# Attention with hash buckets and two MoE layers: weight conversions at other steps, and nine more useless products at the start

## The chip, the core and the metric

The kernel runs on one core of a Trainium2 chip. The metric is the device time of one execution in microseconds (us); smaller is better. Before the change three runs gave 1005.58, 1005.88 and 1007.04 us.

The core has a matrix engine (TensorE, PE in the rows; PEld are its weight loads), VectorE (DVE), ScalarE (ACT), GpSimd (POOL) and SyncE (SP), which only issues DMA transfers. Each engine takes its instructions in the order in which the program wrote them, and waits at an instruction until what it needs is there.

## The reference

```python
B, H, S, D = q.shape                                   # 2, 8, 768, 64
q_bits = (einsum('bhsd,dk->bhsk', q, proj) > 0)        # 6 hash bits of each row
k_bits = (einsum('bhsd,dk->bhsk', k, proj) > 0)
mask = q_bucket[:, :, :, None] == k_bucket[:, :, None, :]
scores = where(mask, q @ k.T / sqrt(D), -1e9)
attn = softmax(scores) @ v
x = attn as (1536 tokens, 512)
h = x @ w_in                                           # 512 -> 2048
x = where(h > 0, h, exp(min(h, 0)) - 1) @ w_out        # 2048 -> 512
p = domain_probs / sum                                 # 4 experts
out = sum over e of p[:, e] * (max(x @ w1[e], 0) @ w2[e])
```

`w_in` and `w_out` come as 64-bit floats and are turned into 32-bit ones on the chip, by integer operations on their two words.

## The kernel before

The attention stage works on eight pairs of heads, one after the other. A pair has 12 steps (six row blocks of 128 for each of its two heads); `g2` counts pairs and `i` steps, and the text writes (2, 3) for step 3 of pair 2. `att_step(u)` writes the instructions of one step in the order of the letters in `ORDER`: C combines the product sums of an earlier chunk, E is an exponential on ScalarE, T and t are transpositions on TensorE, Q the score products of two steps ahead, N the row minimum of these on VectorE, H, h, L and l split the transposed exponentials into a high part (ScalarE) and a low part (VectorE), W converts weights in step 3, M, m and d prepare a later pair, and V is the product with v. There is one score tile, so Q waits for the minimum of the step before.

What is prepared depends on the step. In steps 1 and 2 q of the next pair is transposed, in step 3 its hash bits are computed (the hashing step; in pair 0 step 5), in steps 10 and 11 k of the pair after is transposed. The transposed parts are split by GpSimd (`pool_split`) and brought to their places by SP.

Every third step, at i = 0, 3, 6 and 9, the combination C copies a product sum on ScalarE into the tile `t` (`t1` in the code, one buffer); GpSimd copies (L496) and adds (L500) from it. ScalarE can write it again only when GpSimd has done so. In steps 6 and 7 GpSimd multiplies the result of the last pair (L534) with the reciprocals `rx`, which SP loads in step 3 (`load_rx`, L526).

Beside this, three tiles of `w_in` and `w_out` are converted in the attention stage, tile m in the pairs 2m to 2m+3. `conv_w` gives the operations, each for the two halves 0 and 1: a (ScalarE, absolute value), x, s, t, n, m (VectorE: clamp L286, shift L287, merge L289, mask L291, low word L292) and p (GpSimd, addition L294); S0, S1 split the tile (GpSimd, L311 and L315). The table `PRE` says in which pair (relative to 2m) and step each is written; an entry of step 3 is written at W, all others at the end of the step behind the transfers of `loads_step`. The entry c gives the raw tile free, and `consumed` then issues the load of the next raw tile (L259 and L260) on SP at once. For tile 1, which has a place of its own, c does nothing.

At the start `first()` prepares pair 0. `warm(n)` writes n useless products of a zero tile. `WARM` holds their numbers; `WARM[1]` are those between the transpositions of k and of q. `emit_proj32` builds the small weight tile of the hashing step on GpSimd.

After the attention stage (at about 230 us) come the first MoE layer (L885) and the second (L1083 to L1136), both with TensorE working without a rest.

Of the kernel before, what the change touches and what calls it, by code (L numbers as in the profile page):

```python
# [37 lines left out]
def lsh_attention_moe_kernel(  # L38
# [36 lines left out]
    WA = 3  # L75
    ORDER = "CETHQtNRLhlWMmdV"
    ORDER0 = "EQNwTHtLhlWMmd"
    WARM = (28, 1, 8, 6, 4)
    GL = 0.0
    TAIL = "AoqpBpcpproppqppVVVncxkgogkqffzkffppppfffffffffffffffffoqfffffffff"  # L80

# [37 lines left out]
    def pair(g2):  # L119

        return g2 % B, g2 // B

    def load_qk(g2, nm):
        b, hp = pair(g2)
        t = st_p.tile([P, NJ, 2, D], F32, tag="s" + nm, name="s" + nm)
        x = {"k": k, "q": q}[nm][b, 2 * hp:2 * hp + 2]
        if g2:
            nc.sync.dma_start(out=t, in_=x.rearrange("h (p j) d -> p j h d", j=NJ))
        else:
            t = t.rearrange("p j h d -> p (j h d)").rearrange("p (h j d) -> p h j d", h=2, j=NJ)  # L130
            x = x.rearrange("h (p j) d -> p h j d", j=NJ)
            for js in (slice(0, NJ // 2), slice(NJ // 2, NJ)) if nm == "k" else (slice(0, NJ),):
                nc.sync.dma_start(out=t[:, :, js], in_=x[:, :, js])
        raws[g2, nm] = t
# [17 lines left out]
    def pool_split(hi, lo, x):  # L152
        nc.gpsimd.tensor_scalar(out=hi, in0=x, scalar1=1.0, scalar2=1.0, op0=ALU.mult, op1=ALU.mult)
        nc.gpsimd.tensor_tensor(out=lo, in0=x, in1=hi.bitcast(F32), op=ALU.subtract)
# [28 lines left out]
    def emit_proj32():  # L183
        nc.gpsimd.memset(pj32, 0.0)
        for i in range(2):
            r = slice(i * D, (i + 1) * D)
            for n, sign in enumerate((1.0, -1.0)):
                c0 = i * HB + n * NB
                nc.gpsimd.tensor_scalar(out=pj32[r, c0:c0 + NB], in0=prj[r], scalar1=sign, scalar2=1.0,
                                        op0=ALU.mult, op1=ALU.mult)  # L190
# [3 lines left out]
    def x_tiles(c):  # L194
        if c not in xh:
            xh[c], xl[c] = (xp.tile([P, NT], F32R, tag=f"x{n}{c}", name=f"x{n}{c}") for n in "hl")
        return xh[c], xl[c]
# [172 lines left out]
    def place(g2, nm, par):  # L370


        r = slice(par * D, (par + 1) * D)
        hi, lo = stg[nm + "h"][r].bitcast(F32), stg[nm + "l"][r].bitcast(F32)
        t = (ks_t if nm == "k" else qs_t)[sl(g2, par)].bitcast(F32)
        if nm == "k":
            parts = (t[0:D], hi.unsqueeze(1).to_broadcast([D, 2, S])), (t[D:P, 0], lo)
        else:
            parts = (t[0:D, 0], hi), (t[D:P, 0], hi), (t[0:D, 1], lo)
        for dst, src in parts:  # L380
            nc.sync.dma_start(out=dst, in_=src)
# [7 lines left out]
    def place_bits(g2, nm, par):  # L389
        for half in range(2):  # L390
            src, dst = bits_at(g2, nm, par, half)
            nc.sync.dma_start(out=dst.bitcast(F32), in_=src)
# [136 lines left out]
    def emit_fin(g2, half, by):  # L529
        b, hp = pair(g2)  # L530
        t0 = b * S + half * HS
        uu = u_t[g2][:, half * HS:(half + 1) * HS]
        eng = nc.gpsimd if by.space == uu.space else nc.vector
        eng.tensor_tensor(out=uu, in0=uu, in1=by, op=ALU.mult)  # L534
        pool_split(*(t[:, t0:t0 + HS] for t in x_tiles(hp)), uu)
# [8 lines left out]
    def emit_norm(g2, half, ps):  # L544
        for i in range(UC):
# [12 lines left out]
    EU = 0  # L558
    FIN_AT = (6, 7)
    SIDE_AT = (1, 6)  # L560
    PRE = ((0, 3, "a0"), (0, 6, "a1"), (0, 8, "x0"), (0, 10, "s0"), (1, 1, "t0"), (1, 2, "x1"), (1, 3, "s1"),
           (1, 6, "n0"), (1, 10, "t1"), (2, 1, "m0"), (2, 2, "n1"), (2, 3, "m1"), (2, 4, "p0 p1 c"), (2, 5, "S0"),
           (3, 4, "S1 C"))
    PRE = [{(2 * m + p, {3: 5, 6: 7}.get(i, i) if m + p == 0 else i): nm.split() for p, i, nm in PRE}
           for m in range(NPRE + 1)]
    PRE[NPRE][NPAIR - 1, 2] = PRE[NPRE].pop((NPAIR - 2, 5))
    MSTEP = [None] * PU
# [23 lines left out]
    def loads_step(g2, i):  # L591
        if g2 + 2 < NPAIR and i == L_AT:
            load_qk(g2 + 2, "k")
        if g2 + 1 < NPAIR:
            q0, b0, kq1, _ = (4, 5, 5, 0) if g2 == 0 else PLACE_AT
            if g2 == 0 and i == 1:
                place(g2 + 1, "k", 0)
            if i == q0:
                place(g2 + 1, "q", 0)
                if g2 and g2 + 2 < NPAIR:  # L600
                    load_qk(g2 + 2, "q")
            if g2 and i == b0:
                load_rx(g2 - 1)
            if i == b0:
                for nm in "kq":
                    place_bits(g2 + 1, nm, 0)
            if g2 == 0 and i == b0:
                load_v(1, 1)
                load_qk(2, "q")
            if i == kq1:  # L610
                for nm in "kq":
                    place(g2 + 1, nm, 1)
                    place_bits(g2 + 1, nm, 1)
        elif i == PLACE_AT[1]:
            load_rx(g2 - 1)
        if i == PLACE_AT[3] and g2 + 2 < NPAIR:
            place(g2 + 2, "k", 0)
        if i in FIN_AT and 0 < g2 < NPAIR:
            half = FIN_AT.index(i)
            emit_fin(g2 - 1, half, rx_t[g2 - 1][:, half * HS:(half + 1) * HS])  # L620
        if (g2, i) == (0, 0):
            for r in (slice(0, rows.start), slice(rows.stop, P)):
                nc.sync.dma_start(out=edge_t[r, 20:24], in_=consts[r])
            nc.sync.dma_start(out=dp.rearrange("p (b j) e -> p b j e", b=B),
                              in_=dprobs.rearrange("(b p j) e -> p b j e", b=B, j=NJ))
            loads()
        if g2 == 0 and i == 2:
            split_v(0, 1)
        if g2 + 1 < NPAIR and i in (0, 1) and (g2 or i == 0):
            load_v(g2 + 1, i)  # L630
        if (g2, i) == SIDE_AT:
            load_w(*SIDE)
        if g2 + 1 < NPAIR and i in V_AT:
            split_v(g2 + 1, V_AT.index(i))
# [11 lines left out]
    def first():  # L646
# [7 lines left out]

        warm(WARM[0])
        nc.vector.memset(ident, 0.0)
# [22 lines left out]
        for nm in "kq":  # L679
            los = []  # L680
            for half in range(2):
# [3 lines left out]
                if (nm, half) == ("k", 1):  # L685
                    warm(WARM[1])
                act()
# [36 lines left out]
        bits0("q")  # L724
        warm(WARM[2])
        return warm
# [3 lines left out]
        nc.sync.dma_start(out=t[1][D:KM, 1].bitcast(F32), in_=t[0][KM:KM + HB, 1].bitcast(F32))  # L730

    warm = first()
    emit_proj32()
    split_v(0, 0)
    for u in range(LQ):
        emit_qk(u)
        if u < LN:
            emit_min(u)
    warm(WARM[3])
    for u in range(LE):  # L740
# [11 lines left out]
    def pre_step(g2, i):  # L752
        for m in range(NPRE + 1):
            if (g2, i) in PRE[m]:
                if m not in pre:
                    pre[m] = pre_ops(m)
                for nm in PRE[m][g2, i]:
                    pre[m].pop(nm)()

    def att_step(u):  # L760
# [28 lines left out]
        if u == 0:  # L789
            ops["w"] = lambda: warm(WARM[4])  # L790
        if u == PROBS_AT:
# [613 lines left out]
```

## Time and profile before

| | us |
|---|---|
| median of three runs | 1005.88 |
| the profiled execution | 1006.43 |
| its span, first to last instruction | 1004.6 |
| TensorE busy | 998.1 |
| VectorE busy | 831.2 |
| GpSimd busy | 510.9 |
| ScalarE busy | 501.9 |

The profile is of one execution. A timeline row gives the start, the duration, the engine, the line of the code, the operation and what it writes and reads; in square brackets stands how long its engine was idle before it, and what ended that. A matmul's end is modelled, so a step's length is better read from the starts of weight loads.

### The profile page before, as it was taken

To read this page: it belongs to the slowest core of one execution; us is meant where nothing else is said; L and a number is where in the kernel's file an instruction comes from. 1 tells how busy PE (TensorE), PEld (TensorE's weight loads), DVE (VectorE), ACT (ScalarE), POOL (GpSimd) and SP (SyncE) were. 2 spreads that over 40 slices of the span, in tenths; PEclk is the share of its full clock that TensorE was granted. 3 is DMA by queue.
4 is the path that set the end of the run, shared out by engine and by line. 5 is a ranking of instruction groups with operands and counts; after the bars stand their busy time and mean duration, and the time that the engine had idled before them with its cause. 6 is when DMAs were issued, how large, how long until landed. Compare 5 with 4: busy or idle time off the path is not lost.

```text
span 1004.6 us, 16153 instructions
## 1 busy us (share of the span) xinstructions
PE 998.1 (99%) x5901; PEld 880.4 (88%) x5901; DVE 831.2 (83%) x1276; ACT 501.9 (50%) x988; POOL 510.9 (51%) x464
## 2 busy tenths in 40 slices
PE   9999999999999999999999999999999999999998
PEld 8898988898888888888789999999899999999988
DVE  7999999986898787624477788898998989989895
ACT  6989888886565444435433332333423334233331
POOL 5579797973364545412411244555445554455542
PEclk9999999999999999999999999999999999999999
DMA  8777776550222221100200020110201102011012
GB/s 208 168 169 187 164 163 142 127 171 1 84 84 84 84 80 46 42 1 23 71 25 1 12 95 11 43 43 11 95 12 42 43 11 96 11 44 42 1 43 84
DMA packets 72796, 71.97 MB, mean 72 GB/s; under 512 B 26194, under 2 KB 60790, under 8 KB 72718
## 3 DMA queue, kind: packets, MB, share of 16 engines
q1 hardware_dynamic: 72602, 70.95, 25.7%
q8 instruction: 47, 0.77, 0.3%
q14 instruction: 31, 0.25, 0.1%
q10 hardware_dynamic: 116, 0.00, 0.0%
HBM read 48.92 MB, written 3.21 MB: 52 GB/s over the span
## 4 chain that ended last, share of the span: by engine, by line
PE 51%; issue 5%; POOL 1%; ACT 0%; DVE 0%; POOLq 0%
PE l L1136 23%; PE a L1084 4%; PE r L1084 4%; PE a L1083 4%; PE r L1083 4%; PE a L1085 4%; PE r L1085 4%; POOL h L869 1%; PE l L1241 1%; PE l L885 1%; ACT w L313 0%; PE r L832 0%; PE r L831 0%; PE r L833 0%; DVE w L317 0%
## 5 line engine op out<-in xcount | busy, mean ns | idle before, releaser
L1136 PEld LDWEIGHTS l<-w,op 128*128 128x128 f32 x1932 | 241.0, 189 | 7.2
L1136 PE MATMUL l<-w,op 128*128 128x256 f32 x1932 | 243.0, 281 | 0.0
L1152 POOL TENSOR_TENSOR a<-a,temps 128x512 f32<-128x512 f32 x60 | 91.7, 1528 | 122.3 <-DVE a L1147 122.3
L1018 ACT ACTIVATE op<-hf 128x512 fp32r<-128x512 f32 x119 | 73.2, 626 | 137.7 <-DVE hf L1088 85.1
L885 PE MATMUL l<-h,w 128*128 128x512 f32 x576 | 140.1, 391 | 0.1
L869 POOL TENSOR_TENSOR h<-g,h 128x512 fp32r<-128x512 f32 x44 | 67.0, 1524 | 136.7 <-ACT h L865 95.5
L885 PEld LDWEIGHTS l<-h,w 128*128 128x128 f32 x576 | 107.7, 188 | 24.8 <-POOL h L869 1.3
L1022 DVE TENSOR_TENSOR op<-hf,op 128x512 fp32r<-128x512 f32 x119 | 123.3, 1050 | 4.8 <-ACT op L1018 4.7
L431 DVE TENSOR_SCALAR_CACHE_REDUCE mk<-s 128x768 f32<-128x768 f32 x96 | 91.5, 953 | 12.3 <-PE s L422 9.7
L464 DVE TENSOR_TENSOR ptl<-pt,pth 128x384 fp32r<-128x384 f32 x192 | 97.1, 547 | 1.1 <-ACT pth L467 1.0
L440 ACT ACTIVATE mk<-mk,mn 128x768 f32<-128x768 f32 x96 | 89.9, 937 | 10.8 <-DVE mk L431 10.4
L450 PE MATMUL pt<-cst,mk 128*128 128x128 f32 x576 | 93.9, 272 | 0.0
L467 ACT ACTIVATE pth<-pt 128x384 fp32r<-128x384 f32 x192 | 85.8, 487 | 7.2 <-PE pt L450 6.3
L421 PE MATMUL s<-ks,qs 128*128 128x512 f32 (+1 forms) x192 | 80.1, 439 | 1.3 <-DVE mk L431 1.2
L450 PEld LDWEIGHTS pt<-cst,mk 128*128 128x128 f32 x576 | 72.4, 140 | 8.6 <-ACT mk L440 0.4
L1084 PE MATMUL a<-xl,w 128*128 128x512 f32 x192 | 75.3, 392 | 0.0
L1084 PE MATMUL r<-xl,w 128*128 128x512 f32 x192 | 75.3, 392 | 0.0
L1083 PE MATMUL a<-xh,w 128*128 128x512 f32 x192 | 75.3, 392 | 0.0
L1083 PE MATMUL r<-xh,w 128*128 128x512 f32 x192 | 75.3, 392 | 0.0
L1085 PE MATMUL r<-xh,w 128*128 128x512 f32 x192 | 74.9, 390 | 0.0
L1085 PE MATMUL a<-xh,w 128*128 128x512 f32 x192 | 74.9, 390 | 0.0
L480 PE MATMUL pv<-pth,vs 128*128 128x384 f32 x192 | 72.7, 379 | 0.1
(193 smaller groups left out, 2131.4 us busy)
## 6 DMA issues: line engine op xcount, KB each, us to landing
raw<-in_moe_w_dram SPq DMA_DIRECT2D x32, 512.0 KB
raw<-in_moe_w_in_dram SPq DMA_DIRECT2D x15, 512.0 KB
raw<-in_moe_w_out_dram SPq DMA_DIRECT2D x15, 512.0 KB
ks<-kh SPq DMA_DIRECT2D x15, 384.0 KB
qs<-qh SPq DMA_DIRECT2D x30, 192.0 KB
sq<-in_q_dram SPq DMA_DIRECT2D x8, 384.0 KB
sv<-in_v_dram SPq DMA_DIRECT2D x16, 192.0 KB
pb<-pd SPq DMA_DIRECT2D x12, 256.0 KB
```

The costliest lines, as they stand in the source:

```text
L431: nc.vector.tensor_scalar(out=e_t[u], in0=s_t.pop(u)[:, 0:S], scalar1=MASKED, scalar2=None, op0=ALU.min, op1=ALU.min, accum_out=mn)
L440: nc.scalar.activation(out=e, in_=e, func=ACTF.Exp, bias=mn_t.pop(u), scale=-1.0, accum_out=sums_t[g2][:, j, par:par + 1])
L450: nc.tensor.transpose(pt[:, i * P:(i + 1) * P], e_t[u][:, kb * P:(kb + 1) * P], ident)
L464: nc.vector.tensor_tensor(out=lo, in0=pt, in1=hi.bitcast(F32), op=ALU.subtract)
L467: nc.scalar.activation(out=hi, in_=pt, func=ACTF.Copy)
L885: mm(ps, a, b_, start=(m == 0 and n == 0), stop=(m == GS[g] - 1 and n == 2))
L1022: e.tensor_tensor(out=lo, in0=x, in1=hi.bitcast(F32), op=ALU.subtract)
L1083: mm(ps, wh[:, cs], xh[c][:, ts], start=(c == 0), stop=False)
L1084: mm(ps, wh[:, cs], xl[c][:, ts], start=False, stop=False)
L1085: mm(ps, wl[:, cs], xh[c][:, ts], start=False, stop=(c == NC - 1))
L1136: mm(ps[:, tt * HD:(tt + 1) * HD], a[:, cs], b_[:, k_], start=(n == 0), stop=(n == 11))
L1152: nc.gpsimd.tensor_tensor(out=x, in0=x, in1=keep[nm], op=ALU.add)
```

## The change

Three things are changed. The table `PRE` has other steps for the operations of a conversion: the shift and the last low word leave the hashing step, the clamp leaves step 8; VectorE's ten operations now stand in steps 10 and 11 of the first pair, 1, 2, 4, 5, 10 and 11 of the second and 1 and 2 of the third. The additions p0, p1 and the release c move from step 4 of the third pair into step 3. At the start ten instead of one useless products stand between the transpositions of k and q. And the hashing weights are built in step 2 of pair 0 instead of behind `first()`.

```diff
-    WARM = (28, 1, 8, 6, 4)
+    WARM = (28, 10, 8, 6, 4)
...
-    PRE = ((0, 3, "a0"), (0, 6, "a1"), (0, 8, "x0"), (0, 10, "s0"), (1, 1, "t0"), (1, 2, "x1"), (1, 3, "s1"),
-           (1, 6, "n0"), (1, 10, "t1"), (2, 1, "m0"), (2, 2, "n1"), (2, 3, "m1"), (2, 4, "p0 p1 c"), (2, 5, "S0"),
+    PRE = ((0, 3, "a0"), (0, 6, "a1"), (0, 10, "x0"), (0, 11, "x1"), (1, 1, "s0"), (1, 2, "t0"), (1, 4, "s1"),
+           (1, 5, "n0"), (1, 10, "t1"), (1, 11, "n1"), (2, 1, "m0"), (2, 2, "m1"), (2, 3, "p0 p1 c"), (2, 5, "S0"),
            (3, 4, "S1 C"))
-    PRE = [{(2 * m + p, {3: 5, 6: 7}.get(i, i) if m + p == 0 else i): nm.split() for p, i, nm in PRE}
+    PRE = [{(2 * m + p, {3: 5, 6: 8}.get(i, i) if m + p == 0 else i): nm.split() for p, i, nm in PRE}
...
+        if (g2, i) == (0, 2):
+            emit_proj32()
...
     warm = first()
-    emit_proj32()
     split_v(0, 0)
```

VectorE in steps 1 to 3 of pair 2, before. mk is the row minimum that begins a step, ptl are the two low parts, raw and side the weights, hb the hash bits:

```order
L431 TENSOR_SCALAR mk,mn<-s 128x768
L464 TENSOR_TENSOR ptl<-pt_1227,pth 128x3x128
L464 TENSOR_TENSOR ptl<-pt_1237,pth 128x3x128
L291 TENSOR_SCALAR raw<-side 128x512
L431 TENSOR_SCALAR mk,mn<-s 128x768
L464 TENSOR_TENSOR ptl<-pt_1271,pth 128x3x128
L464 TENSOR_TENSOR ptl<-pt_1283,pth 128x3x128
L292 SCALAR_TENSOR_TENSOR raw<-raw 128x512
L406 TENSOR_SCALAR hb<-m,edge 128x384
```

And after, the same two steps:

```order
L431 TENSOR_SCALAR mk,mn<-s 128x768
L464 TENSOR_TENSOR ptl<-pt_1237,pth 128x3x128
L464 TENSOR_TENSOR ptl<-pt_1247,pth 128x3x128
L292 SCALAR_TENSOR_TENSOR raw<-raw 128x512
L431 TENSOR_SCALAR mk,mn<-s 128x768
L464 TENSOR_TENSOR ptl<-pt_1281,pth 128x3x128
L464 TENSOR_TENSOR ptl<-pt_1293,pth 128x3x128
L406 TENSOR_SCALAR hb<-m,edge 128x384
```

The low word L292 has moved out of the hashing step into step 2, and the mask that stood there has moved to step 11 of pair 1.

SP in steps 2 and 3 of pair 2, before. sq is a load of q, rx the reciprocals, the rows with hb bring hash bits, those of kh to ql the parts of the next head, raw are the weights:

```order
L381 DMA qs_126<-ql 64x768
L128 DMA sq<-in_q_dram 128x12x64
L526 DMA rx<-d 64x6x128 x2
L392 DMA ks_123<-hb 12x384 x2
L392 DMA qs_126<-hb 12x384 x2
L381 DMA ks_124<-kh 64x2x768
L381 DMA ks_124<-kl 64x768
L392 DMA ks_124<-hb 12x384 x2
L381 DMA qs_127<-qh 64x768 x2
L381 DMA qs_127<-ql 64x768
L392 DMA qs_127<-hb 12x384 x2
L259 DMA raw<-in_moe_w_in_dram 128x4x256
```

And after:

```order
L381 DMA qs_126<-ql 64x768
L128 DMA sq<-in_q_dram 128x12x64
L259 DMA raw<-in_moe_w_in_dram 128x4x256
L260 DMA raw<-in_moe_w_out_dram 128x1024
L526 DMA rx<-d 64x6x128 x2
L392 DMA ks_123<-hb 12x384 x2
```

The load of the next raw weights has moved from behind all transfers of step 3 to a place ahead of the first of them. The same happens in pair 6.

VectorE in steps 3 to 5 of pair 3, before; here the second weight tile is converted:

```order
L464 TENSOR_TENSOR ptl<-pt_1715,pth 128x3x128
L287 TENSOR_SCALAR w_1294<-w_1294 128x512
L406 TENSOR_SCALAR hb<-m,edge 128x384
L431 TENSOR_SCALAR mk,mn<-s 128x768
L464 TENSOR_TENSOR ptl<-pt_1754,pth 128x3x128
L464 TENSOR_TENSOR ptl<-pt_1764,pth 128x3x128
L431 TENSOR_SCALAR mk,mn<-s 128x768
L464 TENSOR_TENSOR ptl<-pt_1781,pth 128x3x128
```

And after:

```order
L464 TENSOR_TENSOR ptl<-pt_1724,pth 128x3x128
L406 TENSOR_SCALAR hb<-m,edge 128x384
L431 TENSOR_SCALAR mk,mn<-s 128x768
L464 TENSOR_TENSOR ptl<-pt_1762,pth 128x3x128
L464 TENSOR_TENSOR ptl<-pt_1772,pth 128x3x128
L287 TENSOR_SCALAR w_1308<-w_1308 128x512
L431 TENSOR_SCALAR mk,mn<-s 128x768
L464 TENSOR_TENSOR ptl<-pt_1790,pth 128x3x128
L464 TENSOR_TENSOR ptl<-pt_1800,pth 128x3x128
L291 TENSOR_SCALAR side<-w_1308 128x512
```

The shift L287 has moved from the hashing step to the end of step 4, and the mask L291 stands at the end of step 5 (before, of step 6).

## Rows read from the trace of the kernel before

**Rows 1.** The page: busy time, share of the span and instructions of each engine.

```profile
PE 998.1 (99%) x5901; PEld 880.4 (88%) x5901; DVE 831.2 (83%) x1276; ACT 501.9 (50%) x988; POOL 510.9 (51%) x464
```

**Rows 2.** Waits of weight loads, 16 to 225 us: total us, times, longest.

```profile
PEld s L421 <- DVE mk L431: 3.3, 9, 0.7
```

**Rows 3.** The same from 225 us to the end.

```profile
PEld l L885 <- POOL h L869: 1.3, 3, 0.5
PEld l L885 <- DVE a L904: 0.8, 2, 0.4
```

**Rows 4.** Timeline of weight loads: first score load of four steps of pair 2.

```profile
73.57 0.19 PEld L421 LDWEIGHTS s<-ks,qs 128*128 128x128 f32 x1
...
75.97 0.19 PEld L421 LDWEIGHTS s<-ks,qs 128*128 128x128 f32 x1
...
79.01 0.19 PEld L421 LDWEIGHTS s<-ks,qs 128*128 128x128 f32 x1
...
81.69 0.19 PEld L421 LDWEIGHTS s<-ks,qs 128*128 128x128 f32 x1 [0.56 <-DVE mk L431]
```

**Rows 5.** Timeline of VectorE: a shift in two places, two minima of pair 3.

```profile
39.45 0.42 DVE L287 TENSOR_SCALAR side<-side 128x512 int32<-128x512 int32 x1
...
94.92 1.23 DVE L287 TENSOR_SCALAR w<-w 128x512 int32<-128x512 int32 x1
...
110.49 0.96 DVE L431 TENSOR_SCALAR_CACHE_REDUCE mk<-s 128x768 f32<-128x768 f32 x1
...
112.56 0.96 DVE L431 TENSOR_SCALAR_CACHE_REDUCE mk<-s 128x768 f32<-128x768 f32 x1 [0.17 <-PE s L422]
```

**Rows 6.** Timeline of GpSimd in pairs 2, 3 and 6.

```profile
79.70 2.90 POOL L294 TENSOR_TENSOR side<-side,raw 128x512 f32<-128x512 f32 x2
...
87.20 1.01 POOL L534 TENSOR_TENSOR u<-u,rx 128x384 f32<-128x384 f32 x1 [0.99 <-DMA rx<-d]
...
94.86 1.00 POOL L500 TENSOR_TENSOR u<-u,t 64x384 f32<-64x384 f32 x1
...
108.53 1.28 POOL L315 TENSOR_TENSOR w<-side,w 128x512 fp32r<-128x512 f32 x1
...
192.97 2.57 POOL L294 TENSOR_TENSOR side<-side,raw 128x512 f32<-128x512 f32 x2
...
197.82 1.01 POOL L534 TENSOR_TENSOR u<-u,rx 128x384 f32<-128x384 f32 x1
...
205.41 1.01 POOL L500 TENSOR_TENSOR u<-u,t 64x384 f32<-64x384 f32 x1
```

**Rows 7.** Timeline of SP: issues in pairs 2 and 6.

```profile
80.46 2.04 SPq L526 DMA_DIRECT2D rx<-d  x2
...
93.01 0.45 SPq L259 DMA_DIRECT2D raw<-in_moe_w_in_dram  x1
...
191.68 1.51 SPq L526 DMA_DIRECT2D rx<-d  x2
```

**Rows 8.** Timeline of ScalarE: combinations at the first steps of pairs 3 and 7.

```profile
96.95 0.49 ACT L495 ACTIVATE t<-pv 128x384 f32<-128x384 f32 x1 [0.25 <-PE pv L481]
...
208.07 0.49 ACT L495 ACTIVATE t<-pv 128x384 f32<-128x384 f32 x1 [0.30 <-POOL vs L154]
```

**Rows 9.** First 5 us: busy time by engine; granted clock third from the end.

```profile
0.00:5.00 5.00, 4.01 (x33) 3.89 (x34) 1.44 (x6) 1.84 (x3) 1.50 (x10) 1.00 0.56 151
```

**Rows 10.** Timeline of the start, TensorE and one row of GpSimd.

```profile
0.99 3.17 PE L653 MATMUL pz<-pn 128*128 128x128 bf16 x28 [0.99 <-POOL pn L648]
...
6.42 1.54 PE L349 MATMUL pq<-cst,s 128*128 128x128 f32 x6 [0.76 <-DVE s L668]
7.62 1.63 PE L713 MATMUL hk<-kh,pj 128*128 128x384 f32 x4
...
14.69 0.88 PE L450 MATMUL pt<-cst,mk 128*128 128x128 f32 x6
...
10.14 0.79 POOL L189 TENSOR_SCALAR pj<-prj 64x6 f32<-64x6 f32 x4
```

## The prediction

> **What bounds the kernel now.** I read the busy shares first: TensorE is busy for 99% of the span [rows 1], so only two things can move the end: time in which TensorE stands still for another engine, and time in which its products run slowly. The waits of its weight loads over the attention stage come next. From 16 to 225 us the first score product of a step waits for VectorE's minimum nine times, 3.3 us in all [rows 2]; from 225 us to the end all named waits come to 2.1 us, none of them for a weight conversion of the attention stage [rows 3]. So what the attention stage gains or loses arrives at the end nearly whole, and the changed conversions lie in it.
>
> The step length is read from the first score weight load of each step [rows 4], or from VectorE's minima. A plain step takes 2.07 us (110.49 to 112.56 [rows 5]), a step with three transpositions for the next pair 2.40 (73.57 to 75.97), the hashing step 3.04 (75.97 to 79.01). The step after the hashing step takes 2.68 with a wait of 0.56 in it: the conversion in the hashing step of pair 2 made VectorE late, and TensorE paid one step later. In plain steps VectorE itself waits 0.17 for TensorE [rows 5]. It has that little room there, about half a microsecond in steps with transpositions, and about a whole one in the hashing step, if no conversion stands in it.
>
> A conversion has no fixed price. The shift of one 128x512 tile took 0.42 us at 39.45, and 1.23 at 94.92, where GpSimd had begun an addition of 1.00 us at 94.86: VectorE waited until it was over [rows 5, 6].
>
> **The change part by part.** *Conversions out of the hashing steps and out of step 8.* TensorE's waits for VectorE are the 3.3 us of [rows 2]. They come after the hashing steps, after step 8 and after step 10, and all of those places are emptied or get a cheaper operation. I take the whole: **-3.3**.
>
> *Conversions at the new steps.* Per converted tile pair, six of the ten operations stand beside transpositions with half a microsecond of room, and I price these at 0 to 0.3 us. The second one of a run of two stands at step 11, ahead of a plain step. Two (the shift and the masking) stand in the plain steps 4 and 5, with 0.17 of room for 0.42 of work: VectorE's instructions overlap by some 0.1, so about 0.1 each where GpSimd rests. In pairs 3 and 5 GpSimd splits the weights in step 4. That split ended at 109.81 (108.53 + 1.28) in pair 3, and the moved shift would have started just before 110.49 [rows 5, 6]: a miss by 0.6. If GpSimd is over 0.6 us later than before, the shift meets the split and costs 0.8 more (1.23 - 0.42), with something left over for the masking behind it. I take 2.2 for these two pairs, 0.6 for the rest: **+2.8**, from 0.5 (no meeting) to 4.
>
> *The weight load on SP's queue.* This is the part that decides. The last two operations of a conversion (GpSimd's additions) move from the end of step 4 into step 3. On GpSimd nothing changes by that: they still follow the additions of step 3's combination. But with them goes the release of the raw weights, and the load of the next ones (two DMAs) is issued at once: on SP it now stands ahead of the two loads of the reciprocals rx, and it waits there for GpSimd's additions. It happens in pairs 2 and 6. Behind it in SP's queue wait rx, the hash bits and the copies for the next head; GpSimd, TensorE and nobody else want them, in that order.
>
> Pair 2: the additions ended at 82.60 (79.70 + 2.90) [rows 6]. The weight load takes 1.0 to issue (0.45 for the first of two DMAs [rows 7]), the rx pair 2.04, so rx is issued by 85.6 instead of 82.50 (80.46 + 2.04). GpSimd had waited for rx until 87.20 [rows 6], 4.7 after the issue ended; with the 4.7 it comes at 90.3, **3.1 late**; with a shorter way in a queue that has drained by then (4.1, my lower estimate) 2.5 late. I take 2.6. From rx on GpSimd has no rest before step 10's end: it finished the addition of the last combination at 95.86 (94.86 + 1.00), and ScalarE overwrote the tile which that reads, in the next combination, at 96.95 [rows 6, 8]. So 1.1 us of delay are free. Beyond that ScalarE waits, and queued behind it are the exponentials, which TensorE's transpositions need. Some 0.5 us more is hidden, because ScalarE works that far ahead. Against this, the pair's earlier steps run 0.6 faster, which GpSimd doesn't follow. Cost: 2.6 - 1.1 - 0.5 + 0.6 = **+1.6**.
>
> Pair 6: additions ended at 195.54 (192.97 + 2.57); weight load 1.0, rx 1.51 [rows 7], landing 4.2: 202.2 instead of GpSimd's 197.82, 4.4 late. Free are 208.07 - 206.42 (205.41 + 1.01) = 1.65 [rows 6, 8]. Cost: 4.4 - 1.65 - 0.5 + 0.4 = **+2.7**. For both together I keep 0 to 6: no row of before has rx behind a weight load, so the way through the DMA engines is estimated.
>
> *The start.* The granted clock reads 1.00 in the first 5 us already [rows 9], but six transpositions of one shape take 1.54 us at 6.42 and 0.88 at 14.69 [rows 10]. So I read TensorE at the lower of its two levels (1.2 GHz) at 6.42 and at 2.4 GHz by 14.69; the four hashing products at 7.62 (1.63) belong by their length to the lower one. Before 6.42 it stood idle for 0.76 us, for VectorE's copy of q. Nine more products at 0.113 (3.17 / 28) fill this idle time and can delay q's transpositions by 0.3 at most. If TensorE, without a pause now, gets the full clock ahead of them, they save 0.66 and the hashing products behind them about as much: 1.4 at most. Where the clock rises may differ between runs, so I take half of it: **-0.7**, from +0.3 to -1.4.
>
> The Trainium skill speaks against this term: "TensorE: Matmul & The Clock Gate", Part 4, says that transpositions don't count as TensorE being busy in the way products do. By that the products would stand alone between two runs of transpositions and the term would be about 0, the sum 0.7 higher.
>
> *GpSimd's building of the hashing weights* (0.79 us and a small memset [rows 10]) moves from the start, where GpSimd rests afterwards, to step 2 of pair 0, ahead of a split of v and one of q. It makes these 1 us late; the transfers of q that wait for the split are followed on SP by hash bits that come later still. Price 0; without this cover 1.0.
>
> **The sum.** -3.3 + 2.8 + 1.6 + 2.7 - 0.7 = +3.1. The profiled execution took 1006.43 (span 1004.6 and 1.8 around it), 0.55 above the median of 1005.88. I set the sum on the median: **1009.0 us**.
>
> **The rivals.** *A, the clock doesn't rise earlier* (the skill's rule, above): 1009.7. Against it: the rise came while hashing products followed on transpositions without a pause.
>
> *B, SP's wait is absorbed.* If rx comes at most 1.1 us late in pair 2 and 1.65 in pair 6, ScalarE never waits and the two costs of 4.3 are gone: 1004.7. For it: the sq load that fills the DMA engines ahead of rx has more time to drain. Against it: SP can't issue rx before the additions have ended, and that alone is 3.1.
>
> *C, faster.* As B, and the shift in step 4 of pairs 3 and 5 misses GpSimd's split; this decides at 0.6 us of lag of GpSimd at 109.81. Then new waits cost 0.5 instead of 2.8: -3.3 + 0.5 - 0.7 = -3.5, 1002.4. For it: the hashing step has a whole microsecond of room once it is empty.
>
> **How the numbers follow.** A difference under 0.2% (2.0 us) can't be told from none here. Forecast 0.47 (1007.0 to 1011.8 by its own bounds, a small part of it under 1007.9), A 0.14, B 0.25, C 0.14. Faster 0.14 is C alone; slower is the forecast and A without the part near the bound, 0.59; same 0.27. The range leaves out most of C and the highest costs of SP's wait: 1003.8 to 1011.8.
>
> **What would show it.** In the profile after: SP issues the raw weights before rx in pairs 2 and 6, and GpSimd's multiplication waits for rx until about 90 and 202. ScalarE's copy of a product sum waits for GpSimd at the first step of pairs 3 and 7, with TensorE standing still there for 1.5 us or more. The waits of score products for VectorE after hashing steps are gone; new ones appear in steps 5 and 6 of pairs 3 and 5, with conversions of over 1 us in front of them. q's transpositions at the start take about 0.9 us. The prediction is wrong if rx lands by 88.5 in pair 2, or if ScalarE never waits for GpSimd; then B or C holds.

## The result and the profile after

The changed kernel takes **1015.23 us** (median of five runs, 1012.28 to 1016.20) against 1005.58 for the kernel before (1004.84 to 1007.04): slower, ratio 1.0089 with a 95% interval of 1.0071 to 1.0107. The profiled execution took 1016.20, with a span of 1014.4, 9.8 us longer than before.

The first two rows are the page's busy times and granted clock, the others TensorE's waits of weight loads from 16 to 234 us (total, times, longest).

```profile
PE 1002.6 (99%) x5910; PEld 884.4 (87%) x5910; DVE 828.4 (82%) x1276; ACT 502.6 (50%) x988; POOL 512.4 (51%) x464
PEclk9999999989999999999999999999999999999999
PEld pt L450 <- ACT mk L440: 8.5, 5, 3.9
PEld s L421 <- DVE mk L431: 1.1, 5, 0.3
```

TensorE's waits for VectorE's minimum have shrunk from the 3.3 us of [rows 2] to 1.1. In their place stand waits of transpositions (L450) for ScalarE's exponentials, 8.5 us where the kernel before had 0.4, and one slice of the span shows a lower clock. The same waits before, from 16 to 234 us:

```profile
PEld pt L450 <- ACT mk L440: 0.4, 2, 0.2
```

Where the time went, by the start of TensorE's first score product of a step:

| | before, us | after, us | after against before |
|---|---|---|---|
| first of all | 11.63 | 10.29 | -1.34 |
| pair 3, step 0 | 97.07 | 95.03 | -2.04 |
| pair 3, step 3 | 104.09 | 107.83 | +3.74 |
| pair 6, step 0 | 181.00 | 183.39 | +2.39 |
| pair 7, step 0 | 208.03 | 211.07 | +3.04 |
| pair 7, step 3 | 214.34 | 223.64 | +9.30 |
| span | 1004.6 | 1014.4 | +9.8 |

TensorE gains wherever it is not stopped, and loses all of it and more in two places of three steps each (pairs 3 and 7), and a little at the first step of pair 6. The chain in the first of them, as timelines of SP, GpSimd, ScalarE and TensorE's weight loads (start, duration, in brackets the wait ahead of it):

```profile
81.23 0.38 SPq L259 DMA_DIRECT2D raw<-in_moe_w_in_dram  x1
81.67 0.50 SPq L260 DMA_DIRECT2D raw<-in_moe_w_out_dram  x1
82.21 1.30 SPq L526 DMA_DIRECT2D rx<-d  x2
...
78.62 2.58 POOL L294 TENSOR_TENSOR side<-side,raw 128x512 f32<-128x512 f32 x2
...
89.60 1.02 POOL L534 TENSOR_TENSOR u<-u,rx 128x384 f32<-128x384 f32 x1 [4.78 <-DMA rx<-d]
...
97.36 0.98 POOL L500 TENSOR_TENSOR u<-u,t 64x384 f32<-64x384 f32 x1
...
98.38 0.49 ACT L495 ACTIVATE t<-pv 128x384 f32<-128x384 f32 x1 [3.55 <-POOL u L500]
...
99.83 0.50 PEld L450 LDWEIGHTS pt<-cst,mk 128*128 128x128 f32 x3 [3.13 <-ACT mk L440]
```

SP issues the weights when GpSimd's additions are done, then rx; rx lands at 89.60 instead of 87.20 [rows 6]. GpSimd goes on without a rest until its addition ends at 98.34 (97.36 + 0.98; before 95.86). ScalarE, which must not overwrite that addition's tile, waits 3.55 us, and TensorE stands still for 2.98: so much longer than usual (0.17) is the time between the starts of its last product before the wait and its first behind it. The stops of TensorE in this text are read in this way; the rows give 3.13, the gap between weight loads.

Then comes a loss that the waits don't show. Stretches of 2 us: length, busy time with count of PE, PEld, DVE, ACT and POOL, granted clock, DMA share, GB/s:

```profile
96.00:98.00 2.00, 1.02 (x7) 0.70 (x5) 0.97 (x2) 0.00 (x0) 1.86 (x3) 1.00 0.00 0
98.00:100.00 2.00, 0.17 (x1) 0.17 (x2) 0.41 (x2) 1.62 (x4) 1.92 (x4) 0.75 0.00 0
100.00:102.00 2.00, 2.00 (x8) 1.81 (x9) 1.02 (x2) 1.83 (x5) 1.87 (x3) 0.50 0.00 0
102.00:104.00 2.00, 2.00 (x11) 1.92 (x10) 1.95 (x5) 0.95 (x3) 1.82 (x3) 0.50 0.34 71
104.00:106.00 2.00, 2.00 (x9) 1.81 (x8) 0.97 (x1) 1.59 (x5) 1.83 (x3) 0.54 0.99 197
106.00:108.00 2.00, 2.00 (x17) 1.92 (x16) 1.59 (x4) 1.01 (x3) 0.72 (x2) 1.00 0.78 226
```

The clock falls to 0.50 (1.2 instead of 2.4 GHz) while TensorE stands still and stays there for some 6 us of full work: eight to eleven products per stretch instead of seventeen. The next step, from its first score weight load to that of the step behind it, takes 4.69 us:

```profile
100.32 0.34 PEld L421 LDWEIGHTS s<-ks,qs 128*128 128x128 f32 x1
...
105.01 0.34 PEld L421 LDWEIGHTS s<-ks,qs 128*128 128x128 f32 x1
```

It took 2.50 before; with the parts of its neighbours the slow steps cost 2.8 us. Pair 7 shows the same: rx used at 206.62, ScalarE waits, TensorE stands still for 3.78 us, and slow steps cost 2.5 more. The first row below is the small stop (0.85 us) of pair 6:

```profile
186.08 0.31 PEld L450 LDWEIGHTS pt<-cst,mk 128*128 128x128 f32 x3 [1.01 <-ACT mk L440]
...
206.62 1.01 POOL L534 TENSOR_TENSOR u<-u,rx 128x384 f32<-128x384 f32 x1 [5.57 <-DMA rx<-d]
...
215.22 0.49 ACT L495 ACTIVATE t<-pv 128x384 f32<-128x384 f32 x1 [4.41 <-POOL u L500]
...
216.68 0.50 PEld L450 LDWEIGHTS pt<-cst,mk 128*128 128x128 f32 x3 [3.94 <-ACT mk L440]
```

### The profile page after: what moved, and what is told of

Its sections match the earlier page's. It is cut to its first block, busy times and chain, and to the rows that moved or that the text cites. A ratio compares the mean times of both kernels' runs of the same rounds, so it can differ in the third digit from the quotient of the medians.

```text
span 1014.4 us, 16170 instructions
## 1 busy us (share of the span) xinstructions
PE 1002.6 (99%) x5910; PEld 884.4 (87%) x5910; DVE 828.4 (82%) x1276; ACT 502.6 (50%) x988; POOL 512.4 (51%) x464
## 4 chain that ended last, share of the span: by engine, by line
PE 51%; issue 5%; POOL 1%; ACT 0%; DVE 0%; POOLq 0%
PE l L1137 22%; PE a L1085 4%; PE a L1084 4%; PE r L1085 4%; PE r L1084 4%; PE r L1086 4%; PE a L1086 4%; POOL h L870 1%; PE l L1242 1%; PE l L886 1%; ACT w L313 0%; PE r L833 0%; PE r L832 0%; PE r L834 0%; DVE w L317 0%
## 5 line engine op out<-in xcount | busy, mean ns | idle before, releaser
L450 PE MATMUL pt<-cst,mk 128*128 128x128 f32 x576 | 96.2, 277 | 7.1 <-ACT mk L440 7.1
L450 PEld LDWEIGHTS pt<-cst,mk 128*128 128x128 f32 x576 | 73.6, 142 | 16.8 <-ACT mk L440 8.5
```

Source lines behind the costliest of these rows:

```text
L450: nc.tensor.transpose(pt[:, i * P:(i + 1) * P], e_t[u][:, kb * P:(kb + 1) * P], ident)
```

## The experiments

Ratios are to the kernel before, measured beside the run on the same chip, with 95% intervals in brackets. A ratio is not the ratio of the medians and can differ a little from it.

| run | median, us | ratio |
|---|---|---|
| e2_c3 | 1015.83 | 1.0088 [1.0075, 1.0102] |
| e1_c4 | 1005.12 | 0.9988 [0.9979, 0.9996] |
| e13_c3_pair2 | 1009.71 | 1.0034 [1.0021, 1.0047] |
| e7_rx2 | 1003.42 | 0.9975 [0.9965, 0.9986] |
| e14_wait | 1006.36 | 1.0002 [0.9993, 1.0011] |
| e6_fill | 1017.61 | 1.0117 [1.0103, 1.0130] |
| e9_fill2 | 1012.66 | 1.0070 [1.0057, 1.0082] |
| e16_after | 1014.59 | 1.0086 [1.0072, 1.0100] |
| e17_fill2 | 1012.44 | 1.0062 [1.0049, 1.0075] |
| e3_warm | 1005.31 | 0.9989 [0.9980, 0.9998] |
| e4_conv | 1005.96 | 1.0001 [0.9992, 1.0010] |
| e10_rx2 | 1006.33 | 1.0003 [0.9994, 1.0012] |
| e11_rx2_warm | 1005.32 | 1.0000 [0.9991, 1.0008] |
| e12_proj | 1005.42 | 1.0000 [0.9991, 1.0009] |
| e8_rx2_c4 | 1003.52 | 0.9979 [0.9970, 0.9988] |
| e15_best | 1003.71 | 0.9977 [0.9968, 0.9986] |

### Which part of the change makes the loss

e1_c4 takes one part out of the changed kernel, e2_c3 puts that part alone into the kernel before.

```diff
 e1_c4, on the kernel after (parts of lines)
-           (2, 3, "p0 p1 c")
+           (2, 3, "p0 p1"), (2, 4, "c")
 e2_c3, on the kernel before
-           (2, 3, "m1"), (2, 4, "p0 p1 c")
+           (2, 3, "m1 p0 p1 c")
```

> The changed kernel with one edit: the release c of the raw weights, and with it the load of the next ones, goes back to step 4; GpSimd's additions stay in step 3. So SP issues rx without waiting for GpSimd, as before the change. Theory (the weight load ahead of rx on SP's queue makes rx late, ScalarE waits for GpSimd, TensorE for ScalarE, and TensorE's clock falls behind it): the waits of 2.98 us and 3.78 us at the first steps of pairs 3 and 7 and the slow steps behind them (some 2.8 and 2.4 us) go, and 1015.2 us become about 1003.2 us, 2.4 us less than before the change. Rival (the conversions at their new steps or the earlier additions make GpSimd late, whatever SP does): the two waits stay and the time is above 1011 us.

> The kernel before with one edit: the additions p0, p1 and the release c go from step 4 to step 3, behind the last low word; all other conversions, the start and the hashing weights as before. Theory (SP's queue): the same two waits appear, shorter, because TensorE is not ahead by the 2.0 us that it had gained in the changed kernel: about 1 to 2.5 us each at the first steps of pairs 3 and 7, plus slow steps behind them if such a wait is long enough to bring the clock down; 1008 to 1013 us. Rival (the other moves are needed for the loss): within 1 us of before, 1005.6 us.

Both came out for the theory, though neither in size. Without the early release, 1005.12 us, and no wait of a transposition over 0.2 us; with nothing but the early additions and release, 1015.83, as slow as the whole change and above the 1008 to 1013 expected. So the loss is this one part; the other parts together are worth 1.2 us here, not the 2.4 that I expected.

e2_c3 showed something new: waits at the first step of pairs 3, 4, 5 and 6 (1.44, 1.45, 1.44 and 1.55) and of pair 7 (3.68): the same part, but its loss falls in other places than in the changed kernel. I thought that GpSimd, once late, keeps rx late in the following pairs too, and tested that with the early release in pair 2 alone:

```diff
 e13_c3_pair2, on the kernel before
+    PRE[0][2, 3] += PRE[0].pop((2, 4))
```

> The kernel before with the additions and the release of the raw weights in step 3 for the first weight tile alone (pair 2); pairs 4 and 6 as before. In e2_c3, where all three moved, TensorE waited 1.44 us at the first step of pairs 3, 4 and 5 and 1.55 us of pair 6. Theory (GpSimd, once late, stays late: its splits of q are late, so SP's copies of them, behind which the next rx stands, are late, and it waits for rx again): waits of about 1.4 us at the first steps of pairs 3, 4, 5 and 6, nothing long at pair 7; 4.5 to 6.5 us above before. Rival (each wait has its cause in its own pair): one wait of 1.4 us at pair 3, 1.5 us above before.

The total, 4.5 us above before by the medians (3.4 by the ratio), lies at or under the edge of what I expected, but not in the places that I named. TensorE's waits for ScalarE from 16 to 234 us in e2_c3 (total, times, longest):

```profile
PEld pt L450 <- ACT mk L440: 10.7, 7, 3.8
```

And the same in e13_c3_pair2:

```profile
PEld pt L450 <- ACT mk L440: 4.7, 3, 3.4
```

Pair 3 had one wait of 3.29 us with slow steps behind it, pairs 4 and 5 none, pair 6 one of 0.85. So delay does reach a pair in which nothing was moved (pair 6), but it does not simply stay. Why e2_c3 waited in pairs 4 and 5 and this kernel did not is open; that the long stop in pair 3 let GpSimd catch up fits the numbers, and is only argued. The time has two parts here: in two of the five runs the granted clock reads 1.000 on the mean, and they took 1007.17 and 1007.78 us; in the other three, 0.996 to 0.998, they took 1009.71 to 1009.99.

### Through what rx is late

e7_rx2 leaves the weights where the change put them, and takes rx out of their way:

```diff
 e7_rx2, on the kernel after; in step 3 the two lines are taken out
+            if g2 and i == q0:
+                load_rx(g2 - 1)
             if i == q0:
                 place(g2 + 1, "q", 0)
...
-            if g2 and i == b0:
-                load_rx(g2 - 1)
```

> The changed kernel with one edit: SP issues the reciprocals rx in step 2, ahead of q's copies and of sq, not in step 3; the load of the raw weights still stands in step 3 behind GpSimd's additions. Theory (rx alone carries the delay to GpSimd): rx lands some 4 us before GpSimd wants it, GpSimd no longer waits at its multiplication, the waits of ScalarE and TensorE at the first steps of pairs 3, 6 and 7 go: 1003 to 1004.5 us, as e1_c4. Rival (the weight load delays the hash bits and the copies behind it as well, or GpSimd is late without rx): the waits stay at least in part, above 1007 us.

1003.42 us: the loss is gone, and the kernel beats both others. GpSimd's multiplication in pair 2 no longer waits, and ScalarE's combination waits for a product again, not for GpSimd (e7_rx2, timelines):

```profile
84.39 1.01 POOL L534 TENSOR_TENSOR u<-u,rx 128x384 f32<-128x384 f32 x1
...
94.92 0.49 ACT L495 ACTIVATE t<-pv 128x384 f32<-128x384 f32 x1 [0.25 <-PE pv L481]
```

So rx carries the delay, and nothing else that stands behind the weights does. But the weights can delay rx in two ways: SP waits for GpSimd before it issues them, and their 1 MB lies ahead of rx in the DMA engines. e14_wait keeps the first and takes the second away:

```diff
 e14_wait, on the kernel after
-           (2, 3, "p0 p1 c")
+           (2, 3, "p0 p1 y"), (2, 4, "c")
...
+                y = dram.tile([1, P], F32, tag="y", name="y")
+                nc.sync.dma_start(out=y, in_=w32[0, m][1][0:1, 0:P])
```

> The changed kernel, but in step 3 of pairs 2 and 6 SP issues, in the place of the weight load, a copy of 512 bytes of the weights that GpSimd has just finished (to a place that nobody reads); the weight load itself goes back to step 4. SP waits for GpSimd as in the changed kernel, with nothing large ahead of rx. Theory (the wait decides): rx lands in pair 2 some 4.7 us or less behind the end of its issue at about 82.8 us, that is by 87.5 (89.60 in the changed kernel, 87.20 before, at a TensorE that was 1.3 us later); a wait of 0.5 to 1.5 us at the first step of pair 3, too short for the clock to fall; pair 7 about 3 us; 1009 to 1012 us. Rival (the weights in the DMA engines decide): no wait in pair 3, at most 1 us in pair 7; below 1006.5 us. Rival 2 (all is as long without the weights): 1015 us.

1006.36 us, as fast as before: the rival was right on the greater part, and my theory that SP's wait decides was wrong. But its ratio is 1.0002 where e1_c4, without SP's wait, has 0.9988, so the wait is not free everywhere. SP and GpSimd in pair 2 of e14_wait (timelines):

```profile
81.01 0.25 SPq L752 DMA_DIRECT2D y<-side  x1
81.31 1.29 SPq L526 DMA_DIRECT2D rx<-d  x2
...
85.63 1.01 POOL L534 TENSOR_TENSOR u<-u,rx 128x384 f32<-128x384 f32 x1 [1.02 <-DMA rx<-d]
```

And in e1_c4, whose SP does not wait, with TensorE at the same place to 0.3 us:

```profile
79.38 2.42 SPq L526 DMA_DIRECT2D rx<-d  x2
...
85.69 1.02 POOL L534 TENSOR_TENSOR u<-u,rx 128x384 f32<-128x384 f32 x1 [1.07 <-DMA rx<-d]
```

SP's wait makes the issue of rx begin 1.9 us later (81.31 against 79.38) and end 0.8 later (82.60 against 81.80), and rx is used at the same time: in pair 2 the wait costs nothing. In the changed kernel the issue ended at 83.51 (82.21 + 1.30) and rx was used 6.1 us later, in e14_wait 3.0. The stretch behind the issue in the changed kernel, with the DMA engines' share and rate at its end:

```profile
83.50:86.50 3.00, 3.00 (x22) 2.78 (x21) 2.77 (x8) 3.00 (x8) 1.24 (x2) 1.00 1.07 349
```

And in e14_wait:

```profile
82.60:85.60 3.00, 3.00 (x22) 2.87 (x21) 2.64 (x6) 3.00 (x8) 1.86 (x3) 1.00 0.53 149
```

So of the 4.0 us by which rx is later in the changed kernel, 0.9 are the later end of its own issue, most of that the issue of the weights ahead, and 3.1 its longer way through the DMA engines. The Trainium skill, "DMA: Bandwidth & Descriptors", section "Queues, rings and completion order", says that SP's transfers share one ring on each of 16 engines and that descriptors are consumed in ring order; the trace agrees (3.0 us without the weights ahead, 6.1 with them). It does not tell the order in the rings from DMA engines that are simply busy.

In pair 6 SP's wait does count. Rows of pair 6 in e14_wait, with TensorE's wait at the first step of pair 7 last:

```profile
192.01 2.59 POOL L294 TENSOR_TENSOR side<-side,raw 128x512 f32<-128x512 f32 x2
...
194.97 1.29 SPq L526 DMA_DIRECT2D rx<-d  x2
...
199.20 1.02 POOL L534 TENSOR_TENSOR u<-u,rx 128x384 f32<-128x384 f32 x1 [2.95 <-DMA rx<-d]
...
209.31 0.31 PEld L450 LDWEIGHTS pt<-cst,mk 128*128 128x128 f32 x3 [1.45 <-ACT mk L440]
```

And the same multiplication in e1_c4, which waits for nothing:

```profile
195.37 1.01 POOL L534 TENSOR_TENSOR u<-u,rx 128x384 f32<-128x384 f32 x1
```

GpSimd's wait for rx was 1.07 us in pair 2 and none in pair 6 without SP's wait (e1_c4), 1.02 and 2.95 with it (e14_wait), 4.78 and 5.57 with the weights as well (the changed kernel). So the weights make the whole of the delay in pair 2; in pair 6 a little over half is SP's wait, and e14_wait keeps stops of 0.85 us at pair 6 and 1.29 at pair 7.

### What the low clock costs

The first try put useless products into the two waits, but into a tile that VectorE was still to read, and VectorE waited for ScalarE's combination.

```diff
 e6_fill, on the kernel after (10 in pair 3, 13 in pair 7, ahead of T)
+                    mm(pf[:, 0:P], ident, ident, start=True, stop=True)
 e9_fill2 and e17_fill2, on the kernel after (14 and 18, in a free part of the transposition tile)
+            mm(pt[:, HS:HS + P], ident, ident, start=True, stop=True)
```

> The changed kernel with useless products (the unit matrix with itself, 128x128, about 0.27 us each) in the two long waits: 10 ahead of the transpositions of step 1 in pair 3, and 13 in pair 7. ScalarE, GpSimd and SP do what they did. Theory (the slow steps behind the waits are TensorE's lower clock, which falls because it stands still): TensorE is released at the same time as without them, but the next two steps take their usual 2.07 to 2.52 us: 1015.2 less some 5 us, about 1010 us. Rival (the steps behind the wait are long because the other engines have to catch up): the products change nothing, 1014.5 to 1016 us.

This one tells nothing on its question: its products started at 99.14, when the wait was nearly over, and most of them ran at the low clock (0.50 from 100 to 102); they only added work (e6_fill, timeline of TensorE):

```profile
99.14 3.95 PE L798 MATMUL m<-cst 128*128 128x128 f32 x20 [2.47 <-DVE sums L506]
```

The second try lets them start at once.

> The changed kernel with useless products (the unit matrix with itself) in the two long waits, written into a part of the transposition tile that nobody reads, so that they need not wait for ScalarE: 14 ahead of the transpositions of step 1 in pair 3, 18 in pair 7; at 0.19 us each by the spacing of such products in e6_fill (20 instructions of about 0.094 us at the higher clock for 10) they fill 2.6 of 2.98 and 3.4 of 3.78 us. Theory (TensorE's clock falls because it stands still): the granted clock stays up, the steps behind the waits take their usual length, and 1015.2 us become about 1010 us. Rival (the slow steps come from the other engines catching up): 1015 us.

The products in pair 3 of e9_fill2, and two of the stretches shown above of the changed kernel:

```profile
97.07 3.29 PE L449 MATMUL pt<-cst 128*128 128x128 f32 x28
...
98.00:100.00 2.00, 2.00 (x21) 2.00 (x20) 0.47 (x3) 1.88 (x5) 1.92 (x4) 1.00 0.00 0
100.00:102.00 2.00, 2.00 (x19) 1.90 (x18) 1.53 (x3) 1.82 (x5) 1.83 (x4) 1.00 0.00 0
```

The granted clock stays at 1.00 in the very stretches where it was 0.75 and 0.50, and the step behind takes 2.50 us instead of 4.69 (e9_fill2):

```profile
100.42 0.19 PEld L421 LDWEIGHTS s<-ks,qs 128*128 128x128 f32 x1
...
102.92 0.19 PEld L421 LDWEIGHTS s<-ks,qs 128*128 128x128 f32 x1
```

So the slow steps are TensorE's clock, and it falls because TensorE stands still. The whole time, 1012.66 us, fell by half of what I had expected (1010). For the price at the end both kernels ran again side by side:

> The changed kernel itself again, beside e17_fill2: 1013 to 1016 us, with the same two waits and slow steps.

> The kernel of e9_fill2 again, in one call with the changed kernel. The products keep the clock, as they did in e9_fill2. Theory (the slow steps are lost time of their own): 2.5 to 5 us under e16_after. Rival (what the clock gives back is lost again in TensorE's next waits): within 1 us of e16_after.

1014.59 and 1012.44 us: 2.15 us between the medians, a little under the 2.5 that I expected. In the trace of e16_after the slow steps cost 3.2 us (5.3 in that of the changed kernel, which was the slowest of its five runs), so a part of what the clock gives back is lost again: e17_fill2 has two more waits, which make a step longer by 0.7 in pair 4 and by 0.9 in pair 5.

### What the other parts gain

```diff
 e3_warm, on the kernel before
-    WARM = (28, 1, 8, 6, 4)
+    WARM = (28, 10, 8, 6, 4)
 e4_conv, on the kernel before: the table of the change, with
+           (2, 4, "p0 p1 c")
 e10_rx2: the edit of e7_rx2, on the kernel before; e11_rx2_warm: this and the edit of e3_warm
 e12_proj, on the kernel before
-    emit_proj32()
...
+        if (g2, i) == (0, 2):
+            emit_proj32()
```

> The kernel before with one edit: ten instead of one useless products between the transpositions of k and of q. Theory 1: TensorE is 1.34 us ahead from the first step on, as in the trace of the changed kernel, and nothing takes it back: 1004.2 us. Theory 2: the lead is taken back where ScalarE has little room to GpSimd (1.09 us at the first step of pair 3, 0.24 us of pair 4), because GpSimd waits for rx, which does not come so much earlier: 1004.8 to 1005.4 us.

> The kernel before with VectorE's conversions (and ScalarE's second absolute value in pair 0) at the changed steps, but the additions and the release of the raw weights left in step 4, one useless product at the start and the hashing weights where they were. Theory (moving the conversions is worth the waits that it removes less the new ones, and the run with the release in step 4 shows 1.0 us of it between the first step and step 4 of pair 7): about 1 us less than before in the same call. Rival (the run e1_c4 gained by the start alone): no change within 0.3 us.

> The kernel before with one edit: SP issues rx in step 2, ahead of q's copies and of sq. Conversions, start and release of the raw weights as before. Theory (the kernel before pays nothing for rx; early reciprocals only give room to what is moved on top): TensorE keeps its waits of 3.3 us for VectorE's minimum, time within 0.7 us of before. Rival (rx alone brings the gain of e7_rx2): 2 us or more under before.

> As e10_rx2, with ten useless products between the transpositions of k and of q. Against e7_rx2 only the steps of the conversions and the building of the hashing weights differ. Theory (with rx early, the moved conversions are worth 1 us or more, because their own new waits, 3.9 us in e4_conv, were made by a late GpSimd): about 1.0 us under e10_rx2, and 1 us or more above e7_rx2 measured against the same kernel before (ratio about 0.9985 to 0.999, not 0.9975). Rival (the conversions are worth nothing in any surroundings, as in e4_conv): the same ratio as e7_rx2.

> The kernel before with one edit: GpSimd builds the hashing weights in step 2 of pair 0, not behind the preparation of pair 0. Priced at 0 in the prediction, 1.0 us without cover. Theory: within 0.4 us of before. Rival: 1 us slower, with a wait of the hashing products or of v's split in pair 0.

**The start.** Ten products gain 1.0 us by the medians in both pairs of runs that differ by nothing else (e3_warm against before, e11_rx2_warm against e10_rx2); by the ratios it is 1.1 and 0.3. The traces show how. With one product the first score product started at 11.63, 11.42 and 11.61 us (before, e10_rx2, e4_conv) but at 10.17, 10.05 and 9.81 in e2_c3, e12_proj and e13_c3_pair2; with ten it started between 9.99 and 10.29 in all twelve traces. The products and q's transpositions in the changed kernel (timeline of TensorE):

```profile
5.36 1.27 PE L655 MATMUL pz<-pn 128*128 128x128 bf16 x10
6.42 1.03 PE L349 MATMUL pq<-cst,s 128*128 128x128 f32 x6
```

And q's transpositions in e10_rx2, with one product:

```profile
6.37 1.54 PE L349 MATMUL pq<-cst,s 128*128 128x128 f32 x6 [0.64 <-DVE s L668]
```

With one product the higher clock comes in some executions only among the hashing products; with ten it came before q's transpositions were over each time. That it can come earlier without them too makes the gain differ between runs: the eleven runs of e10_rx2 lie in two groups, 1004.76 to 1005.41 and 1006.33 to 1006.68, those of e11_rx2_warm in one, 1004.90 to 1005.57, and the medians of the kernel before lay between 1005.23 and 1006.30 in the four groups of experiments.

**The conversions.** Alone they gain nothing (e4_conv, ratio 1.0001), early reciprocals alone gain nothing (e10_rx2, 1.0003), and the two together, with ten products, gain 2.6 us (e7_rx2), while reciprocals and products without the conversions stand at 1.0000 (e11_rx2_warm; I had expected 0.9985 to 0.999). Since the start of the kernel before varies, the medians of the kernels with ten products say it more plainly, though they were not measured side by side: 1005.31 us with neither (e3_warm), 1005.32 with early reciprocals (e11_rx2_warm), 1005.12 with the conversions (e1_c4), 1003.42 with both (e7_rx2). TensorE's waits for VectorE's minimum from 16 to 234 us in e4_conv:

```profile
PEld s L421 <- DVE mk L431: 3.6, 10, 1.0
```

In e10_rx2:

```profile
PEld s L421 <- DVE mk L431: 3.3, 9, 0.7
```

And in e7_rx2:

```profile
PEld s L421 <- DVE mk L431: 2.0, 8, 0.3
```

But e1_c4 has as few, with a GpSimd that still waits 6.1 us for rx in pairs 2 to 7:

```profile
PEld s L421 <- DVE mk L431: 2.0, 8, 0.5
```

So the conversions pay with early reciprocals and not without them; that the reciprocals do it by sparing VectorE's waits is not shown, and why the two need each other stays open.

**The hashing weights.** No change (1.0000), as priced.

### Versions that beat both kernels

> As e7_rx2, and the release of the raw weights in step 4 as in e1_c4. Theory: GpSimd loses its last waits for rx (6.1 us in pairs 2 to 7 of e1_c4) and works ahead; TensorE's remaining waits for VectorE's minimum shrink a little, since GpSimd's operations meet other conversions: 1003.5 to 1005 us, at most 1 us under e1_c4. If TensorE's pairs were bound by GpSimd's round from rx to rx, it would be 2 us or more under e1_c4.

```diff
 e15_best, e7_rx2 with
-           (1, 4, "s1"), (1, 5, "n0")
+           (1, 3, "s1"), (1, 4, "n0")
```

> As e7_rx2, with the second shift at step 3 instead of 4 and the first mask at step 4 instead of 5 (the first step behind is then a plain one without a conversion). e7_rx2 had waits for VectorE of 0.22 to 0.30 us at step 6 of pairs 1, 3 and 5 and at step 0 of pairs 2, 4 and 6. Theory (two conversions in two plain steps in a row are what is too much): the three waits at step 6 go, 0.8 us under e7_rx2, about 1002.7 us. Rival (the shift makes the hashing step late again): new waits of 0.3 us at step 4, 1003.4 us or more.

With rx ahead, it no longer matters when the weights are released (e8_rx2_c4, 1003.52; that is 1.6 us under e1_c4 by the medians, where I had expected at most 1). And e15_best, 1003.71, followed its rival: the waits of 0.3 us at step 6 are gone, and as many stand at step 4, behind the hashing step. The best are e7_rx2 and e8_rx2_c4, 2.6 and 2.5 us under before by the medians.

## Why the prediction was wrong

The direction and the places were right: SP issues the weights ahead of rx in pairs 2 and 6, rx comes late, and ScalarE and then TensorE wait at the first steps of pairs 3 and 7. The size was a third of the measured one, and the time lay above the range. Term by term, in the profiled execution:

| term | forecast, us | in the trace, us |
|---|---|---|
| VectorE's waits, new ones less old ones | -0.5 | -2.2 |
| start | -0.7 | -1.3 |
| wait at pair 3 | +1.6 | +3.0 |
| wait at pair 6 | none | +0.9 |
| wait at pair 7 | +2.7 | +3.8 |
| low clock behind the waits | none | +5.3 |
| rest | 0 | +0.3 |
| sum | +3.1 | +9.8 |

- **The low clock was left out.** This is the step that failed by most. The prediction priced a wait at its length, and so put the steps behind it at nothing; they cost 5.3 us in this execution and 3.2 in that of e16_after. (The mean granted clock was 0.993 in this and one other of the five runs and 0.996 in three, as in e16_after; with the lower price the sum would still lie above the forecast.) I had read the two levels of the clock at the start, and used them there, but not asked what a wait of some microseconds does to the clock later on. The waits forecast (1.6 and 2.7 us) would have been shorter than those that brought it down here (3.0 to 3.8); the waits of 1.3 to 1.6 us in e14_wait and e2_c3 were followed by steps of normal length.
- **The gains were added to the waits, though a wait swallows them.** In *pair 2* the prediction let TensorE be ahead by 0.6 us, and took its other gains off the sum elsewhere. TensorE came to pair 3 2.04 us ahead, the start's gain included, to wait for a GpSimd that was 2.48 us late: 2.48 - 1.09 of room + 2.04 = 3.43 for ScalarE (measured 3.55), and 0.57 less for TensorE. With the 2.04 in its place the prediction's own working gives 3.0. What stands ahead of a wait is no gain.
- **rx came when I said by luck.** I forecast 89.8 (87.20 + 2.6) in pair 2 and it came at 89.60, but two errors cancel in this: its issue ended at 83.51, not at 85.6, and its way took 6.1 us, not 4.1 to 4.7. No run shows those 4.1 us, nor the 4.2 of pair 6, for a way behind weights: it took 6.1 in pair 2 and 4.9 in pair 6 (206.62 less the end of the issue at 201.75), and 3.0 and 2.9 without the weights (e14_wait). I had priced the weights by their issue alone and the rest by SP's wait. That step failed in pair 2, where the wait alone costs nothing (e14_wait against e1_c4), and with it rival B's argument against itself ("SP can't issue rx before the additions have ended, and that alone is 3.1"). In pair 6 it holds for a little over half of the delay.
- **Pair 6 was undersized.** rx came 8.8 us later than before (206.62 against 197.82), at a TensorE that was 3.0 later, so 5.8 late instead of the 4.4 plus 0.4 of the sum.
- **The conversions** gained more than forecast in the changed kernel, and nothing alone; why is open. That TensorE's long stops give GpSimd time can't be the whole of it, because e1_c4, with neither long stops nor early reciprocals, has waits of 2.0 us against 3.3 before. The waits of 0.24 and 0.28 us at step 6 of pairs 5 and 3 are where they were forecast, at a quarter of their price of 2.2.
- **The start** came out near its forecast (-0.7; -1.0 alone by the medians, -1.3 between the two traces), and rival A is out: there the products would change nothing. The Trainium skill, "TensorE: Matmul & The Clock Gate", Part 4, from which that rival came, says that transpositions don't count as TensorE being busy in the way products do. No run here tests this by itself; with ten products between two runs of transpositions the higher clock was there before the second run was over in twelve traces of twelve.

## What to carry to other kernels

- A small load for which an engine waits must be issued ahead of large ones on its queue: 1 MB in front made its way 3.1 us longer in pair 2. What a wait ahead of the issue costs depends on the place: one that made the issue begin 1.9 us later cost nothing in pair 2, while in pair 6 SP's wait kept GpSimd idle for 2.95 us. With the small load ahead of everything, another change paid that had gained nothing before; why is open.
- Where a new wait stands on the path, price it as the later of two times: all that was gained ahead of it is lost in it. Then add what TensorE loses in the steps behind, if it stood still for long.

## What the runs showed of the hardware

- A stop of 3.0 to 3.8 us brought TensorE's granted clock to 0.50, and it stayed there for up to 6 us in which TensorE worked without a rest; that cost 1.5 to 2.8 us each time beyond the stop (after, e2_c3, e13_c3_pair2, e16_after). In two of the five runs of e13_c3_pair2 the mean granted clock does not show the fall. Useless products in the stop kept it at 1.00 (e9_fill2, e17_fill2), if what they write is free at once.
- The time from the end of rx's issue to its use by GpSimd in pair 2 was 3.0 us in e14_wait, 4.7 before and 6.1 in the changed kernel, the last with 1 MB of weights issued just ahead.
- The same start code, with one useless product, put the first score product at 9.81 to 10.17 us in three traces and at 11.42 to 11.63 in three others.
